# ScalarE's evictions of the remainder sums of layers three and four in 128 columns instead of 256

## The chip, the cores and the metric

The kernel runs on one core of one Trainium2 chip. The metric is the device time of one execution in microseconds, as the median of several runs. Profiles are taken from one execution, and their times count from the first instruction of that execution.

## The reference

Six layers of a cross network. The batch has 4096 rows of 416 values, all in bf16.

```python
B, F, D, L = 4096, 26, 16, 6
Din = min(F * D, 1024)                  # 416
x0: (B, Din)   ws: (L, Din, Din)   bs: (L, Din)

def reference(x0, ws, bs):
    x = x0
    for l in range(ws.shape[0]):
        x = x0 * (x @ ws[l] + bs[l]) + x
    return x
```

## The kernel before

The kernel keeps x transposed: columns of x lie on the partitions, rows of the batch along the free axis. It writes x of layer l as x0 times a running sum c, where each layer adds its product and bias to c (the first layer adds 1 as well). So a layer takes x @ w from TensorE, adds the bias while ScalarE moves the sum out of PSUM, adds that to c on VectorE, and multiplies c by x0 on VectorE for the next layer's x. The names are CM for c, XM0 for x0, XH for the next x.

The 416 columns are three blocks of 128 (index m or k, 0 to 2) and a remainder of 32. The batch is two halves of 2048 rows (s = 0 and 1), each four groups of 512 (g). For the remainder, the four groups of a half are put side by side on the partitions, 4 x 32 = 128, so a half's remainder is one tile of 128 x 512: CR is its c, XR its x, bR its bias.

Layers are counted from l = 0, so layers three and four are l = 2 and l = 3. Layer one (`first_layer`) and the last layer have loops of their own, and layer five (`feeding_layer`) is written out by hand because it also sends c to the last layer in another layout. Layers two, three and four share one loop. Its body takes the six pairs (s, m) in order, two at a time; I call them A to F. `layer_products` issues A's products (`mm_full`, L209, 48 matmuls, and `mm_row`, L215, the part from the remainder rows, four matmuls), opens B with its four row products, lets A be evicted, and issues B's 48. After A and B the loop calls `rem_pair`, which makes the remainder's own sums: `mm_rem` (L221 and L225, sixteen matmuls for each half) into one PSUM tile named pr, then `ew_rem` for each half. Then C and D, then E and F.

The evictions of A to F are done in `ew_main`: ScalarE reads 1024 columns of a PSUM tile at once (L187), VectorE adds to CM (L188) and multiplies into XH (L189). `ew_rem` is the same for a remainder tile of 512 columns: ScalarE's evictions from pr (L197) in pieces of n columns, then one VectorE add into CR (L203) and one multiplication into XR (L204), each over all 512 columns.

All PSUM tiles come from one pool of four, each of 2 x 512 fp32 for each partition, handed out in turn. A pair takes two tiles, pr takes one. A tile can be written again once the evictions that read it are done. The tiles that ScalarE writes (t) come from a pool of six.

Each engine works through its own instructions in program order: ScalarE's order around the change is the evictions of A and B, those of pr for s = 0 and s = 1, those of C. VectorE's is the adds and multiplications of A and B, the two pairs for the remainder, those of C.

Of the kernel before, what the change touches and what calls it, by code (L numbers as in the profile page):

```python
# [16 lines left out]
def kernel(  # L17
# [16 lines left out]
    CW = 512  # L34
# [45 lines left out]
    def pin(ins):  # L80
        tc.keep_in_program_order(ins)
# [109 lines left out]
    def ew_rem(l, s, pr, nxtR):  # L191
        cols = slice(CW * s, CW * s + CW)
        halves = [slice(a, a + CW // 2) for a in range(0, CW, CW // 2)]
        base = CR[:, cols] if l == 0 else tpool.tile([P, 2 * CW], BF16, name="t")
        n = CW // (4 if s and l in (1, 2) else 2)
        for a in range(0, CW, n):
            nc.scalar.activation(base[:, a:a + n], pr[:, a:a + n], ACT.Identity, bias=bR[:, l:l + 1], scale=1.0)  # L197
        if l == 0:
            for a in halves:
                part = slice(CW * s + a.start, CW * s + a.stop)  # L200
                pin(nc.vector.tensor_tensor(out=nxtR[:, part], in0=CR[:, part], in1=XR[0][:, part], op=ALU.mult))
            return
        nc.vector.tensor_tensor(out=CR[:, cols], in0=base[:, 0:CW], in1=CR[:, cols], op=ALU.add)  # L203
        nc.vector.tensor_tensor(out=nxtR[:, cols], in0=CR[:, cols], in1=XR[0][:, cols], op=ALU.mult)  # L204
# [30 lines left out]
    def first_layer(s):  # L235
# [53 lines left out]
        for m in range(2):  # L289
            ew_main(0, s, m, 1, pb[m], nxt)  # L290
        ew_rem(0, 0, pr[:, 0, :], nxtR)
        ew_main(0, s, 2, 1, pb[2], nxt)
        ew_rem(0, 1, pr[:, 1, :], nxtR)

    bias_setup()
# [4 lines left out]
    def rem_pair(l, cur, curR, nxtR):  # L300
        pr2 = psum.tile([P, 2, CW], FP32, tag="ps", name="pr2")
        for s in range(NS):
            mm_rem(l, s, pr2[:, s, :], cur, curR)
        for s in range(NS):
            ew_rem(l, s, pr2[:, s, :], nxtR)
# [140 lines left out]
    l = LL  # L446
# [150 lines left out]
```

## Time and profile before

| what | value |
|---|---|
| median of 3 runs | 128.73 us (128.63 to 128.79) |
| the profiled execution | 129.13 us |
| its span | 127.3 us |
| TensorE's granted clock | 0.995 |
| L187, ScalarE, 1024 columns of a main tile | 36 of 1114 ns |
| L197, ScalarE, remainder sums of layers two to four | 8 of 256 columns, 472 ns each; 8 of 128 columns, 380 ns each |
| L369, ScalarE, remainder sums of layer five | 4 of 256 columns, 472 ns each |
| L203 and L204, VectorE, 512 columns | 0.42 us each |

The span goes from the first to the last instruction of the profiled execution, and the rest of its 129.13 us lies around it. Durations in such rows go from the start to the end of one instruction; where instructions follow each other closely, the next can start before the last has ended. In the rows, PE is TensorE's matmuls, PEld its weight loads, DVE is VectorE, ACT is ScalarE, POOL is GpSimd and SP is SyncE. A row names the line, the operation, what it writes and reads (out<-in), and the shape. The number behind x counts instructions; a timeline merges neighbours of one line into one row, which then carries the shape of the first.

### The profile page before, as it was taken

How to read it: one execution, taken by the hardware profiler on the slowest of the kernel's cores; microseconds unless marked ns; L12 is line 12 of the kernel's file. 1: busy time of each engine (PE TensorE's matmuls, PEld its weight loads, DVE VectorE, ACT ScalarE, POOL GpSimd, SP SyncE). 2: the span in 40 equal slices, each digit the busy share in tenths (PEclk: the TensorE clock that was granted, in tenths of full speed). 3: DMA queues.
4: the chain of work that ended last, by engine and by line, in shares of the span. 5: the costliest groups of instructions: out<-in, count | busy, mean ns of one | idle time of the engine just before them, and what ended most of it. 6: DMA issues, size and time to landing. Idle time of an engine off the chain costs nothing.

```text
span 127.3 us, 3935 instructions
## 1 busy us (share of the span) xinstructions
PE 122.9 (97%) x1682; PEld 55.2 (43%) x1682; DVE 102.3 (80%) x188; ACT 88.2 (69%) x113; POOL 5.2 (4%) x18
## 2 busy tenths in 40 slices
PE   7999999999999999999999999999999999999980
PEld 3243343354435444534453444344435445445450
DVE  0023679774989898998898998898999999999990
ACT  0047866896869486869485859495859698679760
POOL 4004000500000000000000000000000000000000
PEclk9999999999999999999999999999999999999998
DMA  3999999999880000000000000000049999999865
GB/s 82 238 233 225 186 236 250 306 332 323 253 262 17 5 0 0 8 0 5 0 5 0 5 0 0 5 0 5 0 80 140 197 104 231 171 248 322 268 224 178
DMA packets 42229, 16.37 MB, mean 129 GB/s; under 512 B 31034, under 2 KB 42212, under 8 KB 42212
## 3 DMA queue, kind: packets, MB, share of 16 engines
q1 hardware_dynamic: 37432, 15.40, 53.2%
q10 hardware_dynamic: 4780, 0.72, 3.7%
q8 instruction: 13, 0.21, 0.8%
q14 instruction: 4, 0.03, 0.1%
HBM read 6.15 MB, written 3.41 MB: 75 GB/s over the span
## 4 chain that ended last, share of the span: by engine, by line
PE 88%; DVE 5%; DMA 2%; ACT 1%; DVEq 1%; issue 1%
PE pt L209 50%; PE ph L241 13%; PE py L464 6%; PE pt L215 5%; PE pr L225 5%; PE wps L148 4%; DVE o L505 2%; DVE t L523 2%; DMA out_dram<-XH 2%; PE pr L221 2%; PE ph L248 2%; PE py L458 1%; PE py L477 1%; ACT t L519 1%; DVEq L592 1%
## 5 line engine op out<-in xcount | busy, mean ns | idle before, releaser
L209 PE MATMUL pt<-XH,WM 128*32 128x512 bf16 x1152 | 65.2, 379 | 0.0
L187 ACT ACTIVATE t<-pt,bM 128x1024 bf16<-128x1024 f32 x36 | 37.1, 1114 | 13.1 <-PE pt L215 13.1
L209 PEld LDWEIGHTS <-WM 128*32 128x32 bf16 x1152 | 29.7, 97 | 33.8 <-issue 5.1
L188 DVE TENSOR_TENSOR CM<-t,CM 128x1024 bf16<-128x1024 bf16 x36 | 24.7, 687 | 4.3 <-ACT t L187 4.3
L189 DVE TENSOR_TENSOR XH<-CM,XM 128x1024 bf16<-128x1024 bf16 x36 | 24.9, 692 | 2.6
L464 PE MATMUL py<-WM,XH 128*128 128x416 bf16 x90 | 17.0, 339 | 0.0
L241 PE MATMUL ph<-XM,WM 128*128 128x512 bf16 x72 | 16.5, 381 | 0.0
L333 ACT ACTIVATE t<-pt,bM 128x1024 bf16<-128x1024 f32 x12 | 12.4, 1114 | 4.1 <-PE pt L215 4.1
L181 ACT ACTIVATE CM<-ph,bM 128x1024 bf16<-128x1024 f32 x12 | 12.5, 1112 | 3.5 <-PE ph L248 3.5
L519 ACT CAST t<-py 128x416 bf16<-128x416 f32 (+1 forms) x18 | 10.8, 601 | 3.3 <-PE py L464 1.4
L183 DVE TENSOR_TENSOR XH<-CM,XM 128x512 bf16<-128x512 bf16 x24 | 8.8, 429 | 4.1 <-ACT CM L181 4.1
L464 PEld LDWEIGHTS <-XH 128*128 128x128 bf16 x90 | 8.5, 98 | 7.5 <-issue 1.2
L241 PEld LDWEIGHTS <-WM 128*128 128x128 bf16 x72 | 6.7, 98 | 8.5 <-issue 1.3
L341 DVE TENSOR_TENSOR CM<-t,CM 128x1024 bf16<-128x1024 bf16 x12 | 8.0, 688 | 0.3 <-ACT t L333 0.3
L345 DVE TENSOR_TENSOR XH<-CM,XM 128x2048 bf16<-128x2048 bf16 (+1 forms) x7 | 7.5, 1069 | 0.2
L215 PE MATMUL pt<-XR,WR 32*128 32x512 bf16 x96 | 7.3, 379 | 0.0
L505 DVE TENSOR_TENSOR o<-t,X0rows 128x832 bf16<-128x832 bf16 (+1 forms) x15 | 7.1, 485 | 0.0
L225 PE MATMUL pr<-XH,WM 128*32 128x512 bf16 x96 | 6.6, 379 | 0.0
L523 DVE TENSOR_TENSOR t<-t,XLrows 128x832 bf16<-128x832 bf16 (+1 forms) x13 | 6.5, 502 | 0.0
L197 ACT ACTIVATE t<-pr,bR 128x256 bf16<-128x256 f32 (+1 forms) x16 | 5.3, 426 | 1.6 <-PE pr L225 1.6
L114 ACT ACT_TABLE_LOAD x1 | 1.3, 1283 | 6.2 <-DMA XM<-in_x_dram 6.2
L157 DVE CAST bM<-pb 128x18 f32<-128x18 bf16 x1 | 0.2, 177 | 5.6 <-PE pb L156 5.6
(64 smaller groups left out, 69.7 us busy)
## 6 DMA issues: line engine op xcount, KB each, us to landing
X0rows<-in_x_dram SPq DMA_DIRECT2D x14, 208.0 KB, 4.0
out_dram<-o SPq DMA_DIRECT2D x11, 208.0 KB, 3.7
WM<-in_ws_dram SPq DMA_DIRECT2D x5, 312.0 KB, 6.2
out_dram<-XH SPq DMA_DIRECT2D x4, 208.0 KB, 2.6
WR<-in_ws_dram SPq DMA_DIRECT2D x4, 130.0 KB, 4.0
X0rows<-in_x_dram SPq DMA_DIRECT2D x4, 104.0 KB, 5.8
WM<-in_ws_dram ACTq DMA_DIRECT2D x1, 312.0 KB, 3.4
XM<-in_x_dram SPq DMA_TRANSPOSE x8, 5.1
```

Of the source, the lines that this page charges most:

```text
L181: nc.scalar.activation(c, src, ACT.Identity, bias=bias, scale=1.0)
L187: nc.scalar.activation(t[:], src, ACT.Identity, bias=bias, scale=1.0)
L188: nc.vector.tensor_tensor(out=c, in0=t[:], in1=c, op=ALU.add)
L189: nc.vector.tensor_tensor(out=x, in0=c, in1=XM0[:, m, c0:c0 + 2 * CW], op=ALU.mult)
L209: nc.tensor.matmul(pts[g // 2][32 * q:32 * q + 32, g % 2, :], lhsT=WM[:, l, k, 128 * m + 32 * q:128 * m + 32 * q + 32], rhs=cur[s][:, k, C ...
L215: nc.tensor.matmul(pts[g // 2][:, g % 2, :], lhsT=WR[32 * g:32 * g + 32, l, 128 * m:128 * m + 128], rhs=curR[32 * g:32 * g + 32, CW * s:CW ...
L225: nc.tensor.matmul(pr[32 * g:32 * g + 32, :], lhsT=WM[:, l, k, NK * P:D], rhs=cur[s][:, k, CW * g:CW * g + CW], start=False, stop=(k == NK ...
L241: nc.tensor.matmul(pt[:, gl, :], lhsT=WM[:, 0, k, 128 * m:128 * m + 128], rhs=cur[:, k, c0:c0 + CW], start=(k == 0 and not after_row), sto ...
L333: nc.scalar.activation(ts[t + (h,)][:], pts[t][h][:].rearrange("p a b -> p (a b)"), ACT.Identity, bias=bM[:, t[1], l:l + 1], scale=1.0)
L464: nc.tensor.matmul(py[:, 0:D], lhsT=q_x(q, g, k), rhs=WM[:, l, k, :], start=((not closes) and k == 0), stop=(closes and not adds and k == ...
L505: pin(nc.vector.tensor_tensor(out=o[:, j:j + n, :], in0=src, in1=X0rows[:, rows(q, g0, n), :], op=ALU.mult))
L519: nc.scalar.copy(t[:, n * D:n * D + w * D].rearrange("p (a d) -> p a d", a=w), src)
```

## The change

The width of `ew_rem`'s pieces changes in three places.

```diff
-        n = CW // (4 if s and l in (1, 2) else 2)
+        n = CW // (4 if l and (s or l > 1) else 2)
         for a in range(0, CW, n):
             nc.scalar.activation(base[:, a:a + n], pr[:, a:a + n], ACT.Identity, bias=bR[:, l:l + 1], scale=1.0)
```

CW is 512. Before, a quarter (128 columns, four evictions) was used for s = 1 of layers two and three (l = 1 and 2), and a half (256 columns, two evictions) in the other calls. After, a quarter is used for s = 1 of layer two and for both halves of layers three and four. So s = 0 of l = 2, and s = 0 and s = 1 of l = 3, go from two evictions of 256 columns to four of 128. Layer one (l = 0) keeps 256, and layer five has evictions of its own in `feeding_layer`, which the diff does not touch. The same elements are computed with the same bias; the instructions of the other engines and their order are the same.

## The prediction

> **What bounds the kernel now.** I read the page first, then the chain that ended last piece by piece, then ScalarE's lines by form, then the timeline around the places that the diff touches.
>
> ```profile
> span 127.3 us, 3935 instructions
> ...
> PE 122.9 (97%) x1682; PEld 55.2 (43%) x1682; DVE 102.3 (80%) x188; ACT 88.2 (69%) x113; POOL 5.2 (4%) x18
> ...
> PE 88%; DVE 5%; DMA 2%; ACT 1%; DVEq 1%; issue 1%
> ```
>
> TensorE is busy for 97% of the span and carries 88% of the chain; ScalarE carries 1%. The page's average says little about one stage, so here is the chain through layers three and four (l = 2 and 3), whose pieces follow each other without a hole:
>
> ```profile
> 51.75 0.22 PE pr L221 x4
> ...
> 53.48 2.59 PE pt L209 x48
> 56.07 0.54 PE pt L215 x8
> ...
> 70.99 0.21 PE pr L221 x4
> ...
> 72.72 2.59 PE pt L209 x48
> 75.31 0.54 PE pt L215 x8
> 75.85 5.29 PE pt L209 x96
> ```
>
> The columns are start, length, what. The products of the remainder columns (L221, L225, into the PSUM tile pr) start at 51.75 in layer three and at 70.99 in layer four; between the two TensorE has only matmuls. The list of waits for TensorE alone has one entry in the whole span, 0.8 us at its start, so it waits for no eviction anywhere. ScalarE at the same places:
>
> ```profile
> 53.53 1.87 ACT L197 ACTIVATE t<-pr,bR 128x256 bf16<-128x256 f32 x6 [0.54 <-PE pr L225]
> 56.43 4.13 ACT L187 ACTIVATE t<-pt,bM 128x1024 bf16<-128x1024 f32 x4 [1.03 <-PE pt L215]
> ```
> ```profile
> 72.77 1.56 ACT L197 ACTIVATE t<-pr,bR 128x256 bf16<-128x256 f32 x4 [0.54 <-PE pr L225]
> 75.67 4.13 ACT L187 ACTIVATE t<-pt,bM 128x1024 bf16<-128x1024 f32 x4 [1.33 <-PE pt L215]
> ```
>
> The bracket is ScalarE's idle time before the group and its releaser. In layer three the group is two evictions of 256 and four of 128 columns (x6, named by its first form), in layer four it is four of 256. Behind both groups ScalarE stands idle for 1.03 and 1.33 us, until TensorE closes the next tile.
>
> **The price of one place.** The groups by form give the duration of one, from its start to its end:
>
> ```profile
> L197 ACT ACTIVATE t<-pr,bR 128x256 bf16<-128x256 f32 x8 | 3.2, 472 | 1.6 <-PE pr L225 1.6
> L197 ACT ACTIVATE t<-pr,bR 128x128 bf16<-128x128 f32 x8 | 2.3, 380 | 0.0
> ```
>
> Evictions in a row overlap, so what counts is the step from one start to the next. Layer four's four evictions of 256 take 1.56 us and the last of them about 0.48, so the step is (1.56 - 0.48) / 3 = 0.36. In layer three the four of 128 start at 54.26 and last 1.14 together (a timeline from 54.4 to 55.5 shows them alone), so the step is (1.14 - 0.38) / 3 = 0.25. A place that goes from two of 256 to four of 128 costs ScalarE 4 x 0.25 - 2 x 0.36 = 0.28 us. The diff makes one such place in layer three (s = 0) and two in layer four (s = 0 and 1): 0.28 + 0.56 = 0.84 us of ScalarE time and six instructions more. No DMA, no VectorE instruction and no matmul is added or moved, and ScalarE's order stays.
>
> **What lies on the path.** The new group in layer three ends at 53.53 + 1.87 + 0.28 = 55.68 instead of 55.40; the one in layer four at 72.77 + 7 x 0.25 + 0.38 = 74.90 instead of 74.33. Three things wait for these ends.
>
> First, ScalarE's own next work, the evictions of tile C (L187), is not released before 56.43 and 75.67: cover of 0.75 and 0.77 us is left, and the cost on the path is 0.
>
> Second, TensorE. The pool of PSUM has four tiles in turn. Counted from the products before it (A and B take two each, then pr, then C and D two each), the second tile of D takes pr's place, so its row products (the second four of the eight L215) need the end of all evictions of pr. Those eight last from 75.24 to 75.85 in the timeline, one matmul about 0.38, so the last starts at about 75.47. The evictions end 0.57 us ahead of it (1.14 before the change). In layer three it is 56.00 + 0.61 - 0.38 = 56.23 against 55.68, 0.55 ahead. Cost 0; if this cover were gone, the whole lengthening, 0.84 us, would stand on TensorE's path.
>
> Third, VectorE:
>
> ```profile
> 74.18 0.69 DVE L189 TENSOR_TENSOR XH<-CM,XM 128x1024 bf16<-128x1024 bf16 x1
> 74.78 0.42 DVE L203 TENSOR_TENSOR CR<-t,CR 128x512 bf16<-128x512 bf16 x1
> ...
> 75.58 0.42 DVE L203 TENSOR_TENSOR CR<-t,CR 128x512 bf16<-128x512 bf16 x1
> ```
>
> The add for s = 0 (74.78) needs the first four evictions, which will end at 72.77 + 3 x 0.25 + 0.38 = 73.90; it starts later, behind VectorE's earlier multiplication. The add for s = 1 starts at 75.58, and its data will be there at 74.90: 0.68 us to spare. In layer three it is 56.34 against 55.68. Were that late, the multiplication into XR and then the C adds would queue behind it; VectorE idles 0.36 us ahead of the first C add (76.82), and the next reader of XR is the next layer's first row product, far behind. Cost 0.
>
> **Do the smaller evictions change TensorE's pace?** That is the one cost which no wait shows, and this trace holds the trial. The 48 matmuls beside the evictions, from layer two to layer five:
>
> ```profile
> 34.24:36.83 2.59, 2.59 (x54) 1.13 (x48) 2.52 (x5) 1.87 (x6) 0.00 (x0) 1.00 0.90 244
> 53.48:56.07 2.59, 2.59 (x53) 1.15 (x48) 2.42 (x6) 1.87 (x6) 0.00 (x0) 1.00 0.00 0
> 72.72:75.31 2.59, 2.59 (x52) 1.14 (x48) 2.42 (x6) 1.56 (x4) 0.00 (x0) 1.00 0.03 6
> 91.95:94.54 2.59, 2.59 (x53) 1.15 (x48) 2.59 (x5) 1.56 (x4) 0.00 (x0) 1.00 0.10 20
> ```
>
> Columns: stretch, its length, busy time (count) of PE, PEld, DVE, ACT, POOL, granted clock, DMA share, GB/s. With six evictions (the first two rows) and with four (the last two) the stretch is 2.59 us at a granted clock of 1.00. From one layer's first L221 to the next it is 51.75 - 32.52 = 19.23, 70.99 - 51.75 = 19.24 and 90.23 - 70.99 = 19.24. So a place made of four small evictions moves TensorE by 0.01 us at most, either way, and three by 0.03.
>
> **The sum.** 0 on the path, with 0.03 either way. The profiled execution was 129.13 us, of which 127.3 is the span and 1.8 lies around it; it stands 0.40 over the median 128.73 of the runs shown, which go from 128.63 to 128.79. A change of 0 against 129.13 carries over to the median: 128.73.
>
> The Trainium skill (ScalarE: Activation LUTs, section What ACT_TABLE_LOAD costs) gives an eviction with a bias from memory 280 ns and 0.833 ns a column, with an overlap of 93 ns. As an estimate by that page the step is 0.29 us for 128 columns and 0.40 for 256, where the rows have 0.25 and 0.36; a place would cost 0.38 instead of 0.28, and layer four's group would end at 75.22, still 0.25 before the row product. The rule speaks against cutting evictions up, but by it the sum is 0 as well, with half the margin.
>
> **Rivals.**
>
> *Slower: pr comes free too late for D's second tile.* For it: the margin of TensorE falls from 1.14 to 0.57 us, and anything late here is on the path that carries 88%. It decides when the step is over (75.47 - 72.77 - 0.38) / 7 = 0.33 us. Against it: the same instruction at the same place in the layer before has 0.25. If the small ones stepped like the large ones, 0.36, eight would end at 72.77 + 2.52 + 0.38 = 75.67, 0.20 late, likewise in layer three (56.43 against 56.23): 128.73 + 0.40 = 129.13. With no cover at all: 129.57.
>
> *Faster: the six instructions shift something in the last 14 us.* There the chain leaves TensorE (113.35) and goes over ScalarE, VectorE and the output's DMA, and it holds small pieces of "issue" (a wait for nothing that the profile shows), the longest 0.26 us at 122.87. An instruction fetch (queue 14, one packet of 0.01 MB) falls between 120 and 123 us, and ScalarE's stream is one that could need it; a longer stream puts its fetches earlier against the work. If that removed the longest piece: 128.73 - 0.26 = 128.47. Against it: the pieces stand at VectorE, no ScalarE idle time is put down to issue, and the fetch is one packet among 916 in that stretch. The opposite sign is as open, and is held in the slower case. The Trainium skill (Runtime: NRT & Kernel Launch, section Instruction fetch mechanics) says that crossing a fetch boundary is mostly hidden, which speaks for no change; no view of this trace names the engine that fetched.
>
> *The change doesn't do what it says* (the pieces merged again): excluded as far as a profile can, since eight evictions of 128 columns already stand in this one. The time would be 128.73 too.
>
> **How the numbers follow.** About 0.2%, 0.26 us, is what a measurement of this kernel can tell from no change. Hidden (my forecast, 128.73): 0.76. Late pr, or a shift with a price: 0.14, at 129.0 to 129.1. A shift that helps: 0.10, at 128.47. So faster 0.10, same 0.76, slower 0.14. The range goes from 128.45 (the faster case) to 129.05 (into the slower one, short of its full price).
>
> **What would show it.** In the changed profile, L197 has two t<-pr of 256 columns left (layer two, s = 0) and twenty of 128; the groups at about 53.53 and 72.77 hold eight each, last about 2.14 us and are followed by ScalarE idle time of some 0.75 us that ends with PE pt L215; the two stretches of 48 matmuls stay at 2.59 and the layer step at 19.24; TensorE's waits name no ScalarE. The forecast is wrong if TensorE shows an idle time in front of L215 released by ACT t L197, or if the parts from 113 us on have another length than before.

## The result, and the profile after

The changed kernel takes 129.04 us in the median of 7 runs (129.00 to 129.49), the kernel before 128.71 in 7 runs beside it (128.63 to 128.79). The ratio is 1.0031, with a 95% interval of 1.002 to 1.0042: slower by 0.33 us, where no change was forecast. Four later comparisons, below, give a smaller loss: pooled, their 47 runs of the changed kernel have a mean of 128.88 and the 115 of before beside them a mean of 128.80, a difference of 0.08 with a standard error of 0.03. The ratios here and below are those of the record over all runs of a comparison and need not equal the quotient of the two medians. Two runs at a lower granted clock are left out throughout, one of before (212.00 us at 0.566) and the profiled one of minus2 (145.31 us at 0.856), whose profile isn't used either.

I look first for the loss where the change is. The page of the changed kernel:

```profile
span 127.4 us, 3941 instructions
...
PE 122.8 (96%) x1682; PEld 55.4 (43%) x1682; DVE 102.3 (80%) x188; ACT 89.1 (70%) x119; POOL 5.0 (4%) x18
...
PE 88%; DVE 5%; DMA 2%; ACT 1%; DVEq 1%; issue 1%
```

ScalarE has its six instructions more and is busy for 0.9 us longer, close to the 0.84 summed; the other engines' counts are the same and their busy times within 0.2 us. ScalarE's evictions by form, and its timeline in layers three and four:

```profile
L197 ACT ACTIVATE t<-pr,bR 128x128 bf16<-128x128 f32 x20 | 5.5, 381 | 1.1 <-PE pr L225 1.1
...
L197 ACT ACTIVATE t<-pr,bR 128x256 bf16<-128x256 f32 x2 | 0.8, 470 | 0.5 <-PE pr L225 0.5
```
```profile
53.41 2.17 ACT L197 ACTIVATE t<-pr,bR 128x128 bf16<-128x128 f32 x8 [0.54 <-PE pr L225]
56.31 1.11 ACT L187 ACTIVATE t<-pt,bM 128x1024 bf16<-128x1024 f32 x1 [0.73 <-PE pt L215]
```
```profile
72.65 2.17 ACT L197 ACTIVATE t<-pr,bR 128x128 bf16<-128x128 f32 x8 [0.54 <-PE pr L225]
75.55 1.11 ACT L187 ACTIVATE t<-pt,bM 128x1024 bf16<-128x1024 f32 x1 [0.73 <-PE pt L215]
```

The groups of eight last 2.17 us and leave 0.73 us of idle time that still ends with TensorE's row products. TensorE beside them, by stretches (length, then busy time and count of PE, PEld, DVE, ACT, POOL, granted clock, DMA share, GB/s):

```profile
53.36:55.95 2.59, 2.59 (x52) 1.15 (x48) 2.42 (x6) 2.17 (x8) 0.00 (x0) 1.00 0.00 0
72.60:75.19 2.59, 2.59 (x52) 1.14 (x48) 2.42 (x6) 2.17 (x8) 0.00 (x0) 1.00 0.03 6
```

Both are 2.59 us, as before. In the chain layers three, four and five still begin 19.24 us apart, and TensorE's list of waits names no ScalarE. So the middle of the kernel lost nothing. The difference is at the end. First the page's line for the instruction fetches on queue 14 (packets, MB, share), of before and of the changed kernel:

```profile
q14 instruction: 4, 0.03, 0.1%
```
```profile
q14 instruction: 5, 0.04, 0.1%
```

One fetch more lies inside the span. In the trace's packets it has 8192 bytes and starts at 123.27; before, the fifth started at 128.24, behind the span's end at 127.3. Beside it is SP's next to last output issue, alone in a timeline cut close around it (start, length), of before and after:

```profile
123.53 0.37 SPq L508 DMA_DIRECT2D out_dram<-o  x1
```
```profile
123.39 0.73 SPq L508 DMA_DIRECT2D out_dram<-o  x1
```

It takes 0.73 us instead of 0.37, so SP's last issue starts 0.86 instead of 0.51 us after TensorE's last matmul starts. The transfer that ScalarE issues last of all lands later; the DMA issues of the last 4 us (engine, size, us from issue to landing), of before and after:

```profile
out_dram<-o ACTq DMA_DIRECT2D x1, 104.0 KB, 2.0
```
```profile
out_dram<-o ACTq DMA_DIRECT2D x1, 104.0 KB, 2.3
```

ScalarE issues at the same distance from TensorE's last matmul (0.94 us) and its transfer lands 0.3 later. That is the theory to test, "stream": the six instructions moved a fetch into the tail. Its rival, "evictions": the narrow evictions cost the time by themselves, in a way that the profile hides.

### The profile page after: what moved, and what is told of

Its sections match the earlier page's. It is cut to its first block, busy times and chain, and to the rows that moved or that the text cites. A ratio compares the mean times of both kernels' runs of the same rounds, so it can differ in the third digit from the quotient of the medians.

```text
span 127.4 us, 3941 instructions
## 1 busy us (share of the span) xinstructions
PE 122.8 (96%) x1682; PEld 55.4 (43%) x1682; DVE 102.3 (80%) x188; ACT 89.1 (70%) x119; POOL 5.0 (4%) x18
## 4 chain that ended last, share of the span: by engine, by line
PE 88%; DVE 5%; DMA 2%; ACT 1%; DVEq 1%; issue 1%
PE pt L209 50%; PE ph L241 13%; PE py L464 6%; PE pt L215 5%; PE pr L225 5%; PE wps L148 4%; DVE o L505 2%; DVE t L523 2%; DMA out_dram<-XH 2%; PE pr L221 2%; PE ph L248 2%; PE py L458 1%; PE py L477 1%; ACT t L519 1%; DVEq L592 1%
## 5 line engine op out<-in xcount | busy, mean ns | idle before, releaser
L209 PEld LDWEIGHTS <-WM 128*32 128x32 bf16 x1152 | 29.8, 97 | 33.7 <-issue 5.1
L197 ACT ACTIVATE t<-pr,bR 128x128 bf16<-128x128 f32 (+1 forms) x22 | 6.2, 389 | 1.6 <-PE pr L225 1.6
L225 PEld LDWEIGHTS <-WM 128*32 128x32 bf16 x120 | 3.2, 97 | 3.1
```

What stands on the lines that cost most here:

```text
L209: nc.tensor.matmul(pts[g // 2][32 * q:32 * q + 32, g % 2, :], lhsT=WM[:, l, k, 128 * m + 32 * q:128 * m + 32 * q + 32], rhs=cur[s][:, k, C ...
L225: nc.tensor.matmul(pr[32 * g:32 * g + 32, :], lhsT=WM[:, l, k, NK * P:D], rhs=cur[s][:, k, CW * g:CW * g + CW], start=False, stop=(k == NK ...
```

## The experiments

For each kernel the same numbers are read from its profiled execution. Times are us from the start of TensorE's last matmul, which takes the varying start of the executions out: that matmul starts at 123.48 in this execution of before and anywhere from 123.11 to 123.48 in the five of the changed kernel, so the start alone can move a run by as much as the whole loss. "Added" is how many ScalarE instructions there are over before; "landing" is the end of the last output packet (in the rows above it was the completion signal, which comes later); the last column is the end of the span.

| kernel | added | fetch starts, lasts | SP's next to last issue lasts | SP's last issue starts | landing | span ends |
|---|---|---|---|---|---|---|
| before | 0 | 4.76, 0.44 | 0.37 | 0.51 | 2.44 | 3.78 |
| cancel6 | 0 | 4.71, 0.42 | 0.37 | 0.51 | 2.44 | 3.72 |
| l2only | 2 | 4.39, 0.31 | 0.37 | 0.51 | 2.44 | 3.84 |
| l3only | 4 | 2.42, 0.63 | 0.37 | 0.51 | 2.43 | 3.66 |
| minus2_b | 4 | 2.37, 0.43 | 0.37 | 0.50 | 2.43 | 3.68 |
| minus2_c | 4 | 2.38, 0.45 | 0.37 | 0.51 | 2.43 | 3.78 |
| changed, first profile | 6 | -0.09, 0.70 | 0.73 | 0.86 | 2.74 | 4.04 |
| after_again | 6 | -0.07, 0.69 | 0.72 | 0.86 | 2.73 | 4.03 |
| after_third | 6 | -0.09, 0.56 | 0.58 | 0.72 | 2.60 | 3.90 |
| after_4 | 6 | -0.10, 0.50 | 0.51 | 0.64 | 2.53 | 3.74 |
| after_5 | 6 | 0.23, 0.31 | 0.37 | 0.50 | 2.53 | 3.87 |
| pad6 | 6 | -0.08, 0.51 | 0.54 | 0.67 | 2.58 | 3.79 |
| gap6 | 6 | -0.12, 0.53 | 0.51 | 0.65 | 2.54 | 3.77 |
| gap8 | 8 | -0.14, 0.50 | 0.46 | 0.59 | 2.54 | 3.73 |
| gap12 | 12 | -0.93, 0.31 | 0.37 | 0.51 | 2.50 | 3.73 |

In the seven profiles whose long issue has a fetch beside it, the issue ends 0.14 to 0.16 us behind the end of the fetch (in the changed kernel's first one at 0.77 behind 0.62). Where the fetch had ended before the issue began (gap12), or began 0.19 us into it (after_5), the issue takes 0.37 as in before.

A late landing isn't yet a late end. In these profiles 0.36 to 0.51 us lie between the last output packet and the last completion signal, without any relation to the fetch, and the span ends 0.83 to 0.84 behind that signal (1.01 in l2only). So the six profiles with an undisturbed tail (landing at 2.43 or 2.44) end at 3.66 to 3.84, with a mean of 3.74, and the six whose landing is 0.06 to 0.14 late end at 3.73 to 3.87, with a mean of 3.77: a landing that is 0.1 late drowns in what follows. Only the three with a fetch of 0.56 to 0.70 beside the issue, landing 0.16 to 0.30 late, end later than all the others, at 3.90 to 4.04.

**Six instructions that do nothing, at the start (pad6).** The edit to the kernel before:

```diff
     nc.scalar.activation(dz[:, 1:2], dz[:, 0:1], ACT.Identity, bias=dz[:, 0:1], scale=1.0)
+    for _ in range(6):
+        nc.scalar.activation(dz[:, 1:2], dz[:, 0:1], ACT.Identity, bias=dz[:, 0:1], scale=1.0)
```

> The kernel before (evictions of 256 columns as they were) with six one-column ScalarE activations more at the very start, while ScalarE waits for its first data. They write a scratch value that nothing reads. Theory 'stream': the changed kernel loses its time because ScalarE's instruction stream is six longer, so that an instruction fetch of 8 KB moves from behind the end (128.24 in the profile of before) to 123.27, in front of an SP output issue, which then takes 0.73 us instead of 0.37. It expects 129.04 here (0.33 over before), a fetch on queue 14 near 123.3 and one SP issue of about 0.73. Theory 'evictions': the narrow evictions themselves cost the time. It expects 128.71 here and no such fetch.

Measured: 130.09 us, ratio 1.0106 (1.0093 to 1.0119). The fetch and the long issue are there (0.54 us, not the 0.73 expected), but the time is no test. All six write one column and each waits for the semaphore of the one before, and four of them run behind ScalarE's first copies, 0.33 us apart. So its first eviction starts at 12.94 instead of 11.45, and TensorE's last matmul at 124.68 instead of 123.48. This placing of mine was a bad one; gap6 mends it.

**The three places as changed, six instructions fewer elsewhere (cancel6).** The edit to the changed kernel:

```diff
-        n = CW // (4 if l and (s or l > 1) else 2)
+        n = CW // {0: 1, 1: 2}.get(l, 4)
...
-            for a in range(0, CW, CW // 2):
-                nc.scalar.activation(tr[s][:, a:a + CW // 2], pr2[:, s, a:a + CW // 2], ACT.Identity, bias=bR[:, l:l + 1], scale=1.0)
+            nc.scalar.activation(tr[s][:, 0:CW], pr2[:, s, :], ACT.Identity, bias=bR[:, l:l + 1], scale=1.0)
```

> The changed kernel with its narrow evictions in layers three and four, and six ScalarE instructions taken away elsewhere: the remainder's evictions in layer one and layer five are made of 512 columns instead of 256 (minus two and minus two), and layer two's s = 1 of 256 instead of 128 (minus two). ScalarE's stream is as long as before. Theory 'stream': 128.71, no instruction fetch between 122 and 126 us, the last SP issues at 0.37 to 0.44 us. Theory 'evictions': 129.04, since the three places are as changed.

Measured: 128.88 (128.62 to 129.66) against 128.78, ratio 1.0016 (1.0003 to 1.003). The fetch is behind the end again and the landing is 2.44, as "stream" says, but the time isn't the 128.71 that it expected: the interval leaves 1 out, and the 0.10 us left has no place in the profile that I could find. It has edits of its own in layers one, two and five, so it isn't a clean undoing.

**One and two of the places (l2only, l3only).** The edits to the kernel before:

```diff
-        n = CW // (4 if s and l in (1, 2) else 2)
+        n = CW // (4 if (s and l == 1) or l == 2 else 2)          # l2only
+        n = CW // (4 if (s and l in (1, 2)) or l == 3 else 2)     # l3only
```

> One of the three places alone: s = 0 of layer three, two ScalarE instructions more than before. Theory 'stream': the fetch comes two instructions earlier than in before, still behind the last output issue: 128.71. Theory 'evictions': a third of the loss, 128.82.

> Two of the three places: both halves of layer four, four ScalarE instructions more. Theory 'stream': the fetch comes four instructions earlier than in before, about where ScalarE drains behind its own last output issue (124.8 to 125.3), after all SP issues: 128.71, at most 0.1 more by the fetch's share of the DMA engines. Theory 'evictions': two thirds of the loss, 128.93.

Measured: l2only 128.91, ratio 1.001 (1.0001 to 1.0018); l3only 128.69, ratio 0.9998 (0.9988 to 1.0007), both against 128.78. Two of the three places, with ScalarE's lengthening at its largest, cost nothing, so "evictions" falls there for a loss of 0.33 (it expected 128.93). Against the 0.08 of the later comparisons two thirds would be 0.05, which l3only's interval can't exclude. l2only, expected at 128.71 or 128.82, missed both: its 0.13 is more than either a tail at 2.44 explains or l3only allows; together with cancel6 it says that 0.1 us between two kernels of this kind can come from something that these profiles don't show.

**Six to twelve instructions in ScalarE's idle time (gap6, gap8, gap12), and the changed kernel again.** The edit to the kernel before, with 2, (2, 3, 3) and 4 in the three layers:

```diff
+    spare = big.tile([P, 16], FP32, name="spare")
...
             if n == 0:
                 rem_pair(l, cur, curR, nxtR)
+            for j in range(2 if n == 2 else 0):
+                pin(nc.scalar.activation(spare[:, 4 * l + j:4 * l + j + 1], dz[:, 0:1], ACT.Identity, bias=dz[:, 0:1], scale=1.0))
```

> The changed kernel once more, on the chip of this group and beside the same runs of before. Both theories: 1.002 to 1.004 of before, 0.25 to 0.5 us over it. 'Stream' adds: an instruction fetch near 123.3 in the profile, and the SP issue beside it at 0.5 to 0.75 us instead of 0.37.

> The kernel before with its evictions as they were, and six one-column ScalarE activations more: two in each of layers two, three and four, put between D's and E's evictions, where ScalarE is idle for 1.7 us. They write columns of a scratch tile that nothing reads, each its own column, so that none waits for another. (In the first try with six of them each waited for the last one and held up the start by about 1.2 us.) 'Stream': as the changed kernel, 1.002 to 1.004 of before, with the fetch near 123.3 and one lengthened SP issue. 'Evictions': no change, and no fetch that matters.

> The same with eight (two, three and three). 'Stream': the fetch comes two ScalarE instructions earlier than with six, after the cast that starts at 122.2, so at about 122.5 to 122.7, ahead of the SP issue at 122.8. If a fetch lengthens the issue that follows it, that one takes 0.5 to 0.75 and the next ones come late by up to 0.2: 0.1 to 0.3 us over before. If only the overlap at 123.3 hurts: no loss. 'Evictions': no change.

> The same with twelve (four in each layer). 'Stream': the fetch comes six ScalarE instructions earlier than with six, at about 121 to 121.5, where SP waits for VectorE for 0.7 us before and after its issue at 121.7, so that a lengthened issue has slack behind it: within 0.1 us of before. A loss that grows with the number of instructions (by ScalarE's own time) would give twice that of six instead, 0.6.

In gap6's timeline of ScalarE the added ones lie in idle time, and TensorE still ends what is left of it:

```profile
41.20 0.49 ACT L446 ACTIVATE spare<-dz 128x1 f32<-128x1 f32 x2
43.04 4.13 ACT L188 ACTIVATE t<-pt,bM 128x1024 bf16<-128x1024 f32 x4 [1.34 <-PE pt L216]
```

SP's next to last issue, alone, in gap6 and in gap12:

```profile
123.53 0.51 SPq L511 DMA_DIRECT2D out_dram<-o  x1
```
```profile
123.27 0.37 SPq L511 DMA_DIRECT2D out_dram<-o  x1
```

Six idle instructions put the fetch where the six evictions put it (-0.12 and -0.09 in the table) and lengthen the same issue, with every eviction as it was before; twelve put it 0.8 us earlier, and no issue is lengthened. So where the fetch falls, and with it whether the issue is held up, goes by the length of ScalarE's stream, whatever the instructions do. That this costs the runs time isn't shown by this group: against 128.77, the changed kernel has 128.87 (ratio 1.0005, 0.9991 to 1.002), gap6 128.98 (1.0002, 0.9987 to 1.0018), gap8 128.88 (1.0004, 0.9989 to 1.0019), gap12 128.92 (1.0004, 0.9991 to 1.0018). Every interval holds 1. The changed kernel missed the 0.25 to 0.5 that was expected of it, and gap6 the 1.002 to 1.004 of "stream". gap12, which was to stay within 0.1 us of before, is 0.15 over in the median and 0.05 by the ratio; a loss that doubles with twelve instructions (0.6) is excluded.

gap8's fetch missed its forecast too: it came at 123.17, hardly ahead of gap6's, not at 122.6. By the trace's rows of ScalarE the fetch came behind the 192nd with six instructions more, but behind the 194th in gap8 and the 196th in gap12.

**The size, and the path from the issue to the end (after_third, minus2, issue_act, split45).** minus2 is the changed kernel with layer five's part of cancel6's edit alone; minus2_b and minus2_c below are the same kernel again. The other two:

```diff
-            ew(..., nc.scalar if final and u == 7 else nc.sync,
+            ew(..., nc.scalar if final and u in (5, 7) else nc.sync,      # issue_act, from the changed kernel
...
-            paired = final and u < 6
+            paired = final and u < 4                                      # split45, from the kernel before
```

> The changed kernel a third time, for the size of its loss: 0.33 us in the first comparison, 0.10 in the second. 'Stream': the profile again has a fetch that starts about 0.1 us ahead of the SP issue near 123.4, this issue at 0.5 to 0.75 us, and the last output landing 2.5 to 2.75 us after TensorE's last matmul starts (2.44 in before). The times: 0.1 to 0.4 over before.

> The changed kernel with all its three places, and two ScalarE instructions fewer in layer five (the remainder's evictions of 512 columns instead of 256), so that its stream is four longer than before, not six. 'Stream': the fetch falls behind the last output issue, as with the two places of layer four alone (there 125.8); no SP issue over 0.45, the last landing 2.44 after TensorE's last matmul, and the time within 0.1 us of before. 'Evictions': as the changed kernel.

> The changed kernel with one output transfer, the one that SP issues at 123.39, issued by ScalarE instead. The fetch stays near 123.3. If a fetch lengthens any issue beside it, ScalarE's takes 0.7 and SP's last one, at 123.9, is no longer held up: the last landing at 2.44 to 2.6 after TensorE's last matmul, and half of the loss or more gone. If only SP's issues are lengthened, ScalarE's takes 0.38 and the loss is gone. If the fetch's load on the DMA engines is what costs, not the issue, the loss stays at 2.74.

> The kernel before, with the output pair that SP issues at 123.53 split in two single transfers, so that its first half can go at about 123.33 while the DMA engines are idle (they carry under 50 GB/s from 122.4 to 123.8). This asks whether an earlier issue at this place is worth as much as a late one costs: if the tail is set by when the transfers are issued, 0.1 to 0.2 us under before; if each more issue (0.37 us on SP) eats the gain, no change.

Against 128.77: the changed kernel 128.74 (ratio 1.0003, 0.9994 to 1.0011), minus2 128.66 (0.9996, 0.9987 to 1.0005), issue_act 128.82 (1.0007, 0.9997 to 1.0017), split45 128.98 (1.0022, 1.0011 to 1.0033). The changed kernel missed the 0.1 to 0.4 that was expected of it.

The issue that ScalarE took over, alone in a timeline of issue_act:

```profile
123.41 0.41 ACTq L508 DMA_DIRECT2D out_dram<-o  x1
```

It takes 0.41 us beside a fetch of 0.60 (-0.12 to 0.49), SP's last issue starts at 0.44 and nothing holds it up; the landing is 2.53. That is none of the three outcomes as they stand: the issue is hardly lengthened, as in the second, but the landing is that of the first, 0.09 over before and not 0. In this one profile, then, SP's issue is held up by such a fetch and ScalarE's isn't. How much of the late landing goes with SP's issue can't be read off exactly, as the fetch took another time: the changed kernel has landings of 2.60 with a fetch of 0.56 and 2.73 with 0.69. The span of issue_act ends at 3.91, hardly better than 3.90, and its time is no better either. A landing 0.09 late stands in after_5 too, where the fetch started 0.19 us into the issue and lengthened nothing, and nearly so in gap12 (0.06): with a fetch among the output's packets the landing is a little late without any late issue.

split45 was to gain or to stay the same, and lost. Its premise was wrong as well: in before the DMA engines aren't idle from 122.4 to 123.8, but carry some 300 GB/s from 122.8 to 123.4 and under 100 only from there to 123.8. In its timeline, from 122.95 to 124 (the issue before the pair, then the two halves):

```profile
122.60 1.38 SPq L508 DMA_DIRECT2D out_dram<-o  x3
```

Its first half does go earlier, at -0.06 instead of 0.05, but SP starts its last issue at 0.94 instead of 0.51, and the landing is 2.67 instead of 2.44. No fetch is near. This is the second half of the mechanism without a fetch: SP's last issue is 0.43 us late, the landing 0.23 and the time 0.21 (0.22%). One issue more was needed for it, so it isn't the lateness alone. It also says that before's pairing is right.

**The changed kernel beside the shorter stream, twice more (after_4, minus2_b, after_5, minus2_c).**

> The changed kernel a fourth time, beside a kernel with the same evictions and a stream that is two ScalarE instructions shorter (the next one). 'Stream': over that one by 0.05 to 0.3 us in the median. 'Evictions': as that one, both over before. 'The first comparison caught its runs in an unlucky hour': as that one, and as before, within 0.06 us.

> All three places changed, two ScalarE instructions fewer in layer five, again, for a profile without a throttled clock (the first one's granted clock was 0.856) and for its time beside the changed kernel on one chip. 'Stream': no fetch from 121.9 us to the last output issue, the last landing 2.44 after TensorE's last matmul, time within 0.06 us of before. 'Evictions': as the changed kernel.

> The changed kernel a fifth time, once more beside the kernel with the same evictions and a stream two ScalarE instructions shorter. If the loss of the first comparison (0.33 us) belongs to the kernel, it is over before by 0.2 or more here; if it was of that hour, within 0.1 as in the third and fourth. 'Stream', as the profiles show it: the last landing 0.1 us later than in the shorter one with a fetch of 0.5 us, 0.3 later with one of 0.7.

> All three places changed, two ScalarE instructions fewer in layer five, a third time. 'Stream': no fetch between 122 us and the last output issue, the last landing 2.43 to 2.44 after TensorE's last matmul; under the changed kernel by 0 to 0.1 us in the median.

SP's next to last issue, alone, in after_4 and in minus2_b, whose evictions in layers three and four are the same:

```profile
123.15 0.51 SPq L508 DMA_DIRECT2D out_dram<-o  x1
```
```profile
123.22 0.37 SPq L507 DMA_DIRECT2D out_dram<-o  x1
```

Two ScalarE instructions fewer move the fetch from -0.10 to 2.37, the issue is 0.37 again and the landing is 2.43 instead of 2.53. The times: after_4 128.80 (ratio 1.0006, 0.9992 to 1.002) and minus2_b 128.76 (1.0008, 0.9994 to 1.0021) against 128.80; after_5 128.95 (1.0007, 0.9996 to 1.0018) and minus2_c 128.81 (1.0006, 0.9995 to 1.0017) against 128.79. Pooled, the three of minus2 have a mean of 128.82 in 33 runs, with a standard error of 0.04; the changed kernel's 128.88 lies 0.07 over it, with 0.05 of standard error on the difference. That agrees in sign and size with a landing that is 0.1 to 0.3 later in the profiles, but the times alone would not show it. after_4 lies 0.04 over minus2_b, just short of the 0.05 to 0.3 that "stream" expected, and after_5 0.14 over minus2_c; over before after_5 lies 0.16, between the two outcomes named for it.

All later comparisons together say as little: the kernels whose fetch falls beside SP's next to last issue (the changed one, gap6, gap8) lie 0.10 over the mean of before in 71 runs, those whose fetch falls well behind the last issue (cancel6, l2only, l3only, minus2) 0.06 in 67 runs, with a standard error of about 0.03 each. So the fetch and the late issue are shown in the profiles; that they make up the loss of the timed runs is shown only where an execution was profiled with a long fetch in it.

## Why the prediction was right and wrong, point by point

- **ScalarE's price.** Right: 0.84 us were summed, 0.9 measured; a group of eight was to last 2.14 and lasts 2.17, a step of 0.26 where 0.25 was put.
- **The three covers.** Right. ScalarE keeps 0.73 us of idle time (0.75 forecast), TensorE waits for no eviction, and the stretches stay at 2.59. The estimate by the Trainium skill (ScalarE: Activation LUTs, section What ACT_TABLE_LOAD costs), 0.25 us of margin left instead of 0.57, was too strict: the trace has 0.53, since the group ends about where the rows said. (By that estimate a place costs 0.37, not the 0.38 that was written.)
- **TensorE's pace beside small evictions.** Right: the layer step is 19.24 with eight.
- **The step that failed** is the sentence "No DMA, no VectorE instruction and no matmul is added or moved". One DMA was moved, an instruction fetch, from 4.76 us behind TensorE's last matmul to 0.09 ahead of it. No view names the engine that fetched; that it was ScalarE's stream is read from the runs, where the fetch moves with the number of ScalarE's instructions. So the sum of 0 lacked a term: 0.1 to 0.3 us at the landing, as the five profiles of the changed kernel show it (2.53 to 2.74 against 2.44), of which 0 to 0.3 reaches the end of the span.
- **The rivals.** The late pr never happened. The faster rival named the right thing, a fetch moved by six instructions, with the wrong sign as its main case and the wrong fetch: the one at 121.5 us that I pointed to stayed where it was, and the one that mattered was not in the span of before at all. I gave the sign that came true no price of its own; it was put away in the slower case under the price of the late pr. That the range still holds 129.04 is therefore luck: its upper end came from the late pr.
- **The sign that failed to show.** The parts of the chain from 113 us on were to have another length if the forecast was wrong. They have the same, 11.04 us before and 11.05 after, because its last piece is VectorE's queue at the end of the program (DVEq L592, 0.68 us in both) and not the output's landing. The count of fetches and the DMA issues showed what it didn't.
- **The rule on fetches** in the Trainium skill (Runtime: NRT & Kernel Launch, section Instruction fetch mechanics), that a boundary is mostly hidden, holds for the fetches in the middle (one at 51.6 us before and at 51.7 after, without a trace in any wait) and not for one in the last 4 us, where the profile after has an issue of 0.73 us beside it.
- **The size.** The first comparison's 0.33 us is not settled. In the profile the longest fetch explains 0.26 of it at the end of the span (4.04 against 3.78), and all 7 runs of that comparison lie over all 7 of before. The four later ones give 0.10, -0.03, 0.00 and 0.16 in the medians. Runs with a timed result only don't show the fetch, so whether it was long in all seven of the first, whether something else added to it, or whether its runs met an unlucky hour, stays open; so does the 0.1 us of l2only and cancel6, whose tails are undisturbed. No version that I tried beats both kernels: minus2, the nearest, is the same as before.

## What to carry to other kernels

An instruction that is fully hidden on its own engine still lengthens that engine's stream, and here the stream was fetched by DMA in blocks of 8192 bytes: where the last block's fetch falls can be part of a change's price when the kernel ends in a chain of output transfers. Here it was at most 0.3 us of 129, and only when the fetch took long. Count instruction fetches inside the span before and after (a line of the page), and look at the issues beside the last one. To test whether a small loss comes from what instructions do or from how many there are, put as many idle ones where the engine waits anyway.

## What the runs showed of the hardware that was not expected

A fetch of 8192 bytes that took 0.50 to 0.70 us and started 0.12 to 0.19 us ahead of SP's output issue went with an issue of 0.46 to 0.73 us instead of 0.37 (seven profiles), which ended 0.14 to 0.16 us behind the fetch. An issue by ScalarE at the same place took 0.41 beside a fetch of 0.60 (one profile). A fetch of 0.31 us lengthened none, but it also lay elsewhere, 0.19 us into the issue (after_5) or ended before it (gap12). The same fetch of the same program took between 0.31 and 0.70 us in five executions. The fetch came at nearly the same place of ScalarE's stream each time, behind 191 to 196 of its recorded instructions: 4.76 us after TensorE's last matmul with none added, 2.4 with four, and about 0.1 ahead of it with six (0.23 behind it in after_5).
